# Which engine casts the first feed-forward products out of PSUM: ScalarE instead of VectorE in the first batch

## The chip, the cores and the metric

The kernel runs on one core of a Trainium2 chip. The metric is the device time of one execution in microseconds. The core has engines that run side by side, each working through its own queue in order: TensorE (PE; its weight loads are shown apart as PEld), VectorE (DVE), ScalarE (ACT), GpSimd (POOL) and SyncE (SP, which here issues transfers). They wait for one another through semaphores. TensorE writes its results to PSUM, an accumulator memory of eight banks per partition, and another engine has to read them out before a bank can be used again.

## The reference

Attention over hash buckets, followed by a feed-forward layer with a maximum of three products. There are 4 batches, 8 heads, 768 rows and 64 columns per head; every query attends only to the keys whose six sign bits (of a random projection) equal its own.

```python
q_bits = (np.einsum('bhsd,dk->bhsk', q, proj) > 0).astype(np.int64)
k_bits = (np.einsum('bhsd,dk->bhsk', k, proj) > 0).astype(np.int64)
...
scores = scale * np.matmul(q, k.transpose(0, 1, 3, 2))
scores = np.where(mask, scores, -1000000000.0)
...
attn = np.exp(scores)
attn = attn / (np.sum(attn, axis=-1, keepdims=True) + 1e-09)
out = np.matmul(attn, v)
...
h = np.maximum(np.maximum(x @ w1, x @ w2), x @ w3)
return (h @ w_out).astype(np.float32)
```

Here x is the attention output with the heads laid side by side: 3072 rows of 512; h has 768 columns.

## The kernel before

The queries are worked off in nine chunks: three of 256 queries in the first batch (`THIRD`), then two of 384 (`HALF`) in each of the other three. A chunk and a head are split into units: a unit is 768 columns of scores, three blocks of 256 in the first batch and two of 384 afterwards. There are 192 units, 48 in each batch.

**Scores.** For a unit, `scores` issues the score matmuls on TensorE (L298) into one of two score buffers in PSUM (`sc`), and one exponential on ScalarE (L306) that reads the whole buffer and writes a tile `AT`. As there are two buffers, the scores of a unit can start only when the exponential two units before has read its buffer.

**Bursts.** When four heads of a chunk are done, `burst` issues the sums of the exponentials (L358), their reciprocals on VectorE (L365 to L369), and the products with the values (L380); VectorE scales the result into `xT` (L387). From the fourth chunk on VectorE adds the exponentials up first (L329, L332).

**Feed-forward.** `ffn_groups` turns a finished chunk into a list of jobs. The first eighteen are products of a 128-column block `fb` of h with one of the three weights `wi`: four matmuls (L413) into one of four PSUM banks. What reads the bank depends on `wi`: for `wi` 0 the product is cast to float16 into a new tile `ht` (the lines that the change touches, L417 to L420); for `wi` 1 and 2 VectorE takes the maximum with `ht` in place (L422). In chunk 0 all six `wi` 0 jobs come first; in the others the three jobs of a block follow each other, so a cast comes with every third job. Then come the output products (L457), copied out by ScalarE (L461) and sent off by SyncE.

**Order.** It is written out by hand: each engine's instructions stand in its queue in the order in which the program issues them. The main loop runs over the units. For unit `u` it issues first the scores and the exponential of unit `u + 1`, then whatever is due at `u` (transposes of later inputs on VectorE at L202, loads, hashes), then the next feed-forward job or jobs, then bursts. One job falls due per unit in the first batch, 1.15 per unit after it. So a feed-forward job's matmuls stand on TensorE behind the scores of the next unit, and an instruction on ScalarE that reads the product stands behind the exponential of that unit and ahead of the exponential of the one after.

The jobs of chunks 0, 1 and 2, the first batch's, are worked off from 42 to 109 us, during the later units of the first batch and the units of the second. Their products are 256 columns wide, those of the other chunks 384.

Of the kernel before, what the change touches and what calls it, by code (L numbers as in the profile page):

```python
# [17 lines left out]
def kernel(  # L18
# [12 lines left out]
    nc = tc.nc  # L31
# [4 lines left out]
    HALF = S // 2  # L36
# [53 lines left out]
    def bank():  # L90
        i = free_banks.pop(0)
        return i, bank_tiles[i]

    def give(i):
        if i is not None:
            free_banks.append(i)
# [182 lines left out]
    def block_of(b, m):  # L279
        return 2 * (m % MH) + m // MH if b == 0 else m  # L280
# [34 lines left out]
    def xt_of(c):  # L315
        if c not in xts:
            xts[c] = x_pool.tile([P, NJC, HALF], FP16, tag="xT", name="xT")
        return xts[c]
# [83 lines left out]
    def ffn_groups(c):  # L402
        b, q0, w = chunks[c]
        xt = xt_of(c)
        hts, gs, l2 = {}, [], {}
        jobs = [(fb, wi) for fb in range(NFB) for wi in range(3)]
        if c == 0:
            jobs = [(fb, wi) for wi in range(3) for fb in range(NFB)]
        for fb, wi in jobs:
            def go(fb=fb, wi=wi):  # L410
                k_, ps = bank()
                for jc in range(NJC):
                    nc.tensor.matmul(ps[:, 0:w], w_sb[wi][:, jc, fb * P : (fb + 1) * P], xt[:, jc, 0:w],  # L413
                                     start=(jc == 0), stop=(jc == NJC - 1))
                if wi == 0:
                    hts[fb] = h_pool.tile([P, HALF], FP16, tag="ht", name="ht")
                    if w == HALF:  # L417
                        nc.scalar.copy(hts[fb][:, 0:w], ps[:, 0:w])  # L418
                    else:
                        nc.vector.tensor_copy(hts[fb][:, 0:w], ps[:, 0:w])  # L420
                else:
                    nc.vector.tensor_tensor(out=hts[fb][:, 0:w], in0=hts[fb][:, 0:w], in1=ps[:, 0:w], op=AluOp.max)  # L422
                give(k_)
            gs.append(go)
        rows = out[b * S : (b + 1) * S, :].rearrange("(p c) m -> c p m", c=NM)

        def out_rows(tb):
            if c < NCH - 1:
                return o_pool.tile([P, DM], FP32, tag="osb", name="osb")
            if "end" not in nat:  # L430
                nat["end"] = nat_pool.tile([P, 4 * NM * D], FP32, tag="nat", name="nat")
            return nat["end"][:, tb * DM : (tb + 1) * DM]

        def last(tb, cs, use_act):
            k_, ps = bank()
            n = cs.stop - cs.start
            for fb in range(NFB):
                nc.tensor.matmul(ps[:, 0:n], hts[fb][:, tb * P : (tb + 1) * P], wout_sb[:, fb, cs],  # L438
                                 start=(fb == 0), stop=(fb == NFB - 1))
            osb = out_rows(tb)  # L440
            if use_act:
                nc.scalar.copy(osb[:, cs], ps[:, 0:n])
            else:
                nc.vector.tensor_copy(osb[:, cs], ps[:, 0:n])
            give(k_)
            (nc.scalar if use_act else nc.sync).dma_start(rows[block_of(b, q0 // P + tb)][:, cs], osb[:, cs])

        def item(tb, part):
            def go2(part, tb=tb):
                if c == NCH - 1 and tb == w // P - 1:  # L450
                    last(tb, slice(part * DM // 2, (part + 1) * DM // 2), part == 0)
                    return
                if part == 0:
                    l2[tb] = bank()
                k_, ps = l2[tb]
                for fb in range(part * MH, (part + 1) * MH):
                    nc.tensor.matmul(ps[:, 0:DM], hts[fb][:, tb * P : (tb + 1) * P], wout_sb[:, fb, :],  # L457
                                     start=(fb == 0), stop=(fb == NFB - 1))
                if part == 1:
                    osb = out_rows(tb)  # L460
                    nc.scalar.copy(osb[:, 0:DM], ps[:, 0:DM])  # L461
                    give(k_)
                    nc.sync.dma_start(rows[block_of(b, q0 // P + tb)], osb[:, 0:DM])
            gs.append(lambda: go2(part))

        ntb = w // P
        steps = [(0, 0)]
        for tb in range(1, ntb):
            steps += [(tb, 0), (tb - 1, 1)]
        steps.append((ntb - 1, 1))  # L470
        if c == NCH - 1:
            steps = steps[:-3] + [steps[-2], steps[-3], steps[-1]]
        for tb, part in steps:
            item(tb, part)
        return gs
# [194 lines left out]
```

## Time and profile before

| | |
|---|---|
| median of three timed runs | 264.56 us (264.42 to 264.79) |
| the profiled execution | 264.41 us, span 262.4 us |
| TensorE matmul busy | 256.5 us (98% of the span) |
| VectorE busy | 207.8 us (79%) |
| ScalarE busy | 177.9 us (68%) |
| GpSimd busy | 69.8 us (27%) |
| granted TensorE clock | 1.000 |

The span runs from the first to the last instruction of the profiled execution; its time is some 2 us longer. A line such as "L306 ACT ACTIVATE AT<-sc 128x768 ... x192 | 152.4, 816 | 57.2" is a group: line of the program, engine, operation, what it writes and reads, shape and count, then its busy time in us, the mean of one in ns, and how long the engine had been idle just ahead of these instructions, with what ended that. A line of a timeline begins with the start in us and the duration in us; neighbouring instructions of one kind are merged, with their count after the x, and an idle time before them stands in brackets with what ended it. Instructions of one engine can overlap, so the next may start before the last one's duration is over; and since matmuls are pipelined, a group of them shows as longer than the time until the next group begins. Busy shares are averages over stages with different limits.

### The profile page before, as it was taken

What the parts mean: (1) busy time and instruction counts of PE and PEld (TensorE: products, weight loads), DVE (VectorE), ACT (ScalarE), POOL (GpSimd) and SP (SyncE); (2) the same over time, 40 slices, a digit from 0 to 9 for tenths busy, and PEclk for the clock granted to TensorE, in tenths of its full rate; (3) what the DMA queues carried; (4) which work ended last, traced back from release to release, by engine and by line L of the source; (5) the groups of instructions that cost most, each with busy time, mean ns of one, the idle gap of its engine ahead of it and who ended that gap; (6) DMA issues with size and microseconds to landing.
All of it is one profiled execution on the core that took longest, in us unless ns stands there. A gap on an engine that the chain in (4) does not pass through costs nothing.

```text
span 262.4 us, 6477 instructions
## 1 busy us (share of the span) xinstructions
PE 256.5 (98%) x2503; PEld 154.4 (59%) x2503; DVE 207.8 (79%) x492; ACT 177.9 (68%) x258; POOL 69.8 (27%) x132
## 2 busy tenths in 40 slices
PE   8999999999999999999999999999999999999995
PEld 4655658865765666555555554655555555555552
DVE  2897767966799999969999996899849795888350
ACT  3797886667968675956869588584886859581322
POOL 3878752355043526330141612011000000000000
PEclk9999999999999999999999999999999999999999
DMA  6998999979732964970073653802030003000303
GB/s 210 326 224 170 170 235 226 217 132 204 187 91 75 202 139 61 273 186 17 0 198 104 116 127 49 210 0 58 20 122 1 0 2 121 2 0 2 120 0 120
DMA packets 20717, 30.95 MB, mean 118 GB/s; under 512 B 2608, under 2 KB 15248, under 8 KB 20688
## 3 DMA queue, kind: packets, MB, share of 16 engines
q0 software_dynamic: 8128, 13.37, 27.3%
q1 hardware_dynamic: 12128, 16.66, 22.0%
q10 hardware_dynamic: 432, 0.52, 0.6%
q8 instruction: 19, 0.31, 0.5%
q14 instruction: 10, 0.08, 0.1%
HBM read 25.17 MB, written 6.29 MB: 120 GB/s over the span
## 4 chain that ended last, share of the span: by engine, by line
PE 89%; DVE 5%; ACT 3%; issue 2%; DVEq 0%; ACTq 0%
PE ms L413 34%; PE sc L298 22%; PE ms L457 11%; PE ms L380 10%; PE ms L221 3%; ACT AT L306 3%; PE ms L358 3%; PE ms L171 1%; PE ms L123 1%; PE ms L504 1%; DVE ht L422 1%; DVE ad L329 1%; DVE xT L387 1%; PE ms L150 1%; PE ms L438 1%
## 5 line engine op out<-in xcount | busy, mean ns | idle before, releaser
L306 ACT ACTIVATE AT<-sc 128x768 f16<-128x768 f32 x192 | 152.4, 816 | 57.2 <-PE sc L298 53.9
L413 PE MATMUL ms<-xT,w_sb 128*128 128x384 f16 (+1 forms) x648 | 115.0, 307 | 0.3 <-DVE xT L387 0.2
L298 PE MATMUL sc<-S 72*128 72x384 bf16 (+1 forms) x432 | 93.8, 308 | 1.2 <-ACT AT L306 0.9
L413 PEld LDWEIGHTS <-w_sb 128*128 128x128 f16 x648 | 62.7, 97 | 35.9 <-issue 0.4
L422 DVE TENSOR_TENSOR ht<-ht,ms 128x384 f16<-128x384 f16 (+1 forms) x108 | 54.2, 503 | 20.7 <-PE ms L413 10.5
L298 PEld LDWEIGHTS <-S 72*128 72x128 bf16 (+1 forms) x432 | 39.4, 98 | 31.8 <-issue 11.8
L207 POOL TENSOR_SCALAR T<-T 128x768 bf16<-128x768 f32 x24 | 22.8, 951 | 90.2 <-issue 48.4
L457 PE MATMUL ms<-wout_sb,ht 128*128 128x512 f16 x138 | 35.5, 378 | 0.0
L380 PE MATMUL ms<-AT,vo 128*32 128x385 f16 (+3 forms) x840 | 34.2, 308 | 0.0
L380 PEld LDWEIGHTS <-vo 128*32 128x32 f16 x864 | 22.9, 96 | 9.2 <-issue 1.7
L329 DVE TENSOR_TENSOR ad<-ad,AT 128x768 f16<-128x768 f16 x48 | 26.6, 553 | 2.1 <-ACT AT L306 1.3
L202 DVE STREAM_TRANSPOSE T<-nat 128x384 f32<-128x384 f32 x48 | 26.8, 564 | 0.0
L329 DVE TENSOR_TENSOR ad<-AT,AT 128x768 f16<-128x768 f16 x48 | 26.2, 546 | 0.2 <-ACT AT L306 0.2
L418 ACT CAST ht<-ms 128x384 f16<-128x384 f32 x36 | 17.3, 480 | 8.1 <-PE ms L413 8.1
L457 PEld LDWEIGHTS <-ht 128*128 128x128 f16 x138 | 13.3, 97 | 13.0 <-issue 0.3
L387 DVE SCALAR_TENSOR_TENSOR xT<-ms,sv,rb 128x384 f16<-128x384 f32 (+1 forms) x35 | 19.2, 565 | 1.3
L461 ACT COPY osb<-ms 128x512 f32<-128x512 f32 x21 | 12.2, 586 | 7.5 <-PE ms L457 5.8
L332 DVE TENSOR_TENSOR ad<-ad 128x384 f16<-128x384 f16 x32 | 15.5, 484 | 1.1
L137 POOL TENSOR_SCALAR S<-T 64x384 bf16<-64x384 f32 (+1 forms) x23 | 14.1, 616 | 4.9 <-DVE T L132 3.3
L196 POOL DMA_DIRECT2D nat<-in_q_dram x20 | 11.1, 560 | 0.1
L365 DVE STREAM_TRANSPOSE ys<-ms 128x384 f32<-128x384 f32 (+1 forms) x17 | 9.0, 531 | 2.3 <-PE ms L358 2.0
L176 DVE TENSOR_SCALAR S<-ms 6x384 bf16<-6x384 f32 x16 | 8.9, 554 | 2.0 <-PE ms L171 1.2
(52 smaller groups left out, 122.6 us busy)
## 6 DMA issues: line engine op xcount, KB each, us to landing
out_dram<-osb SPq DMA_DIRECT2D x21, 256.0 KB
S<-T SPq DMA_DIRECT2D x48, 96.0 KB
nat<-in_q_dram POOLq DMA_DIRECT2D x20, 192.0 KB, 6.3
vo<-in_v_dram POOLq DMA_DIRECT2D x8, 384.0 KB, 5.8
nat<-in_k_dram POOLq DMA_DIRECT2D x16, 192.0 KB, 5.7
w_sb<-in_moe_w_dram POOLq DMA_DIRECT2D x3, 768.0 KB, 12.8
nat<-in_k_dram SPq DMA_DIRECT2D x10, 192.0 KB
nat<-in_k_dram SPq DMA_DIRECT2D x3, 384.0 KB
```

The lines of the kernel that those rows point to most:

```text
L202: nc.vector.transpose(t32[name][:, u, half * HALF : (half + 1) * HALF], i_)
L207: nc.gpsimd.tensor_scalar(out=t16[name][:, u, :], in0=t32[name][:, u, :], scalar1=RS, scalar2=1.0, op0=AluOp.mult, op1=AluOp.mult)
L298: nc.tensor.matmul(views[j], s_of[kn][0 : D + bits, kx, m * P : (m + 1) * P], s_of[qn][0 : D + bits, qx, q0 : q0 + w], start=True, stop=True)
L306: nc.scalar.activation(t[:, :, 0:w], whole, ActFn.Exp, bias=-SCALE * 0.25 * bits, scale=SCALE)
L329: nc.vector.tensor_tensor(out=sum_of[c, h][:], in0=t[0], in1=t[n], op=AluOp.add)
L332: nc.vector.tensor_tensor(out=t[:, 0, :], in0=t[:, 0, :], in1=t[:, 1, :], op=AluOp.add)
L380: nc.tensor.matmul(av[Q * x : Q * (x + 1), 0:n], v_at[2 * b + i][:, x, cb * D + side : (cb + 1) * D : 2], weights_of(c, 4 * i + x, m)[:, 0 ...
L387: nc.vector.scalar_tensor_tensor(out=xt_of(c)[:, 2 * i + side, 0:w], in0=av[:, 0:w], scalar=sv_of[b, i, side][:], in1=rb[0][:, 0:w], op0=A ...
L413: nc.tensor.matmul(ps[:, 0:w], w_sb[wi][:, jc, fb * P : (fb + 1) * P], xt[:, jc, 0:w], start=(jc == 0), stop=(jc == NJC - 1))
L418: nc.scalar.copy(hts[fb][:, 0:w], ps[:, 0:w])
L422: nc.vector.tensor_tensor(out=hts[fb][:, 0:w], in0=hts[fb][:, 0:w], in1=ps[:, 0:w], op=AluOp.max)
L457: nc.tensor.matmul(ps[:, 0:DM], hts[fb][:, tb * P : (tb + 1) * P], wout_sb[:, fb, :], start=(fb == 0), stop=(fb == NFB - 1))
```

## The change

In the first batch's chunks the cast of the `wi` 0 product out of PSUM is issued on ScalarE and no longer on VectorE. In the other chunks it was on ScalarE before. Eighteen instructions of 128x256 change their engine; nothing else is moved, and the tile that they write and the bank that they read are the same.

```diff
                 if wi == 0:
                     hts[fb] = h_pool.tile([P, HALF], FP16, tag="ht", name="ht")
-                    if w == HALF:
-                        nc.scalar.copy(hts[fb][:, 0:w], ps[:, 0:w])
-                    else:
-                        nc.vector.tensor_copy(hts[fb][:, 0:w], ps[:, 0:w])
+                    nc.scalar.copy(hts[fb][:, 0:w], ps[:, 0:w])
                 else:
                     nc.vector.tensor_tensor(out=hts[fb][:, 0:w], in0=hts[fb][:, 0:w], in1=ps[:, 0:w], op=AluOp.max)
                 give(k_)
```

## The prediction

> **What bounds the kernel now.** I read the page first, then the busy time by windows, then what TensorE waited for, then the engines' timelines around the eighteen casts. From the page, the span and TensorE's total; one digit of the other rows is a fortieth of the span (6.56 us), in tenths busy:
>
> ```profile
> span 262.4 us, 6477 instructions
> ...
> PE   8999999999999999999999999999999999999995
> ...
> DVE  2897767966799999969999996899849795888350
> ACT  3797886667968675956869588584886859581322
> ```
>
> TensorE (PE) is full from the second slice to the last but one. VectorE (DVE) is in tenths 6 to 9 and ScalarE (ACT) 5 to 9 in the slices that hold the casts (7th to 17th, 43 to 105 us): each has room on the average. Waits of TensorE between 40 and 110 us, in total only this:
>
> ```profile
> PE ms L413 <- DVE xT L387: 0.2, 1, 0.2
> ```
>
> and two windows, each with its length and PE, PEld, DVE, ACT and POOL busy: the six casts of chunk 0, and a later stretch with casts of chunk 2:
>
> ```profile
> 43.00:47.50 4.50, 4.50 (x42) 3.82 (x40) 3.79 (x10) 4.50 (x7) 1.28 (x2) 1.00 1.19 239
> 86.00:100.50 14.50, 14.50 (x161) 9.53 (x163) 14.12 (x37) 10.14 (x14) 5.42 (x8) 1.00 0.67 148
> ```
>
> So the time is set by TensorE's own stream. An edit away from TensorE can gain only the little that TensorE loses to others, and it costs whatever it makes TensorE wait. VectorE's 14.12 of 14.50 us looks like the bound, but TensorE is at 14.50 of 14.50: VectorE is late there without holding anybody up. The first window is the opposite: ScalarE has 4.50 of 4.50, and that is where six casts go within seven exponentials.
>
> **What the change removes and adds.** Eighteen casts of 128x256 leave VectorE and join ScalarE's in-order queue, each right behind the exponential of the unit issued just before the product; matmuls, banks, transfers and the order of everything else stay. Group rows:
>
> ```profile
> L306 ACT ACTIVATE AT<-sc 128x768 f16<-128x768 f32 x192 | 152.4, 816 | 57.2 <-PE sc L298 53.9 <-POOL AT L395 2.1
> ...
> L418 ACT CAST ht<-ms 128x384 f16<-128x384 f32 x36 | 17.3, 480 | 8.1 <-PE ms L413 8.1
> ...
> L420 DVE CAST ht<-ms 128x256 f16<-128x256 f32 x18 | 7.4, 411 | 3.3 <-PE ms L413 3.3
> ...
> L442 ACT COPY nat<-ms 128x256 f32<-128x256 f32 x1 | 0.4, 372 | 0.1
> ```
>
> VectorE is relieved of 7.4 us, which is worth nothing except where TensorE waits for VectorE. ScalarE takes 18 casts of about 0.37 us (L442: same engine, same size, f32 out). What counts is the time that a cast adds between two exponentials, since neighbours overlap:
>
> ```profile
> 22.25 1.51 ACT L306 ACTIVATE AT<-sc 128x768 f16<-128x768 f32 x2 [0.69 <-PE sc L298]
> ...
> 123.95 0.81 ACT L306 ACTIVATE AT<-sc 128x768 f16<-128x768 f32 x1 [0.17 <-PE sc L298]
> 124.66 0.47 ACT L418 CAST ht<-ms 128x384 f16<-128x384 f32 x1
> 125.02 0.83 ACT L306 ACTIVATE AT<-sc 128x768 f16<-128x768 f32 x1
> ```
>
> Two exponentials take 1.51, so the second starts 0.70 to 0.71 after the first (1.51 - 0.81; 124.66 - 123.95). A cast of 384 columns adds 0.36 (125.02 - 124.66). The 256-column copy is 0.108 shorter than the 384-column cast (0.480 - 0.372): c = 0.25 us. Bounds: 0.24 if the 0.36 shrinks with the width (0.36 x 256/384), 0.37 if nothing overlaps. I take 0.25, since every such pair in the rows overlaps.
>
> The Trainium skill, "ScalarE: Activation LUTs", section "What ACT_TABLE_LOAD costs", gives an ACTIVATE with immediate scale and bias 186 ns + 0.833 ns per column, neighbours overlapping by 93 ns: c would be 0.31 (186 + 213 - 93), an estimate from that page. The trace's 384-column cast is a little under that formula (0.480 against 0.506); with 0.31 the sum below would be +1.07 instead of +0.65.
>
> **First stretch, chunk 0.** TensorE alternates score matmuls (L298) and one product (L413); ScalarE is close behind:
>
> ```profile
> 42.83 0.49 PE L298 MATMUL sc<-S 70*128 70x256 bf16 x3
> 43.16 0.60 PE L413 MATMUL ms<-xT,w_sb 128*128 128x256 f16 x4
> 43.59 0.49 PE L298 MATMUL sc<-S 70*128 70x256 bf16 x3
> ...
> 46.67 0.49 PE L298 MATMUL sc<-S 70*128 70x256 bf16 x3
> 47.00 0.60 PE L413 MATMUL ms<-xT,w_sb 128*128 128x256 f16 x4
> ```
>
> A unit takes TensorE 0.76 to 0.77 (43.59 - 42.83). On ScalarE:
>
> ```profile
> 41.91 6.09 ACT L306 ACTIVATE AT<-sc 128x768 f16<-128x768 f32 x8 [3.03 <-PE sc L298]
> ...
> 42.62 2.37 ACT L306 ACTIVATE AT<-sc 128x768 f16<-128x768 f32 x3
> ```
>
> ScalarE needs 0.71 for an exponential; with a cast 0.96, more than TensorE's 0.77. Two score buffers let TensorE run two units ahead, then the scores of a unit wait for the exponential two before it, starting 0.04 after it ends:
>
> ```profile
> 31.28 0.81 ACT AT L306
> ...
> 32.13 0.49 PE sc L298 x3
> ```
>
> Call the eight exponentials E1 to E8; E2 starts at 42.62. One cast follows each of E2 to E7; its product is always done by then (the first by 43.03, against 43.33 when ScalarE is free), so ScalarE runs without a gap. E6 starts at 42.62 + 4 x (0.707 + c), ends 0.81 later, and the scores of E8 (46.67 now) may start at 46.30 + 4c: 4c - 0.37 late, 0.63 us. After E8 TensorE has the sums and values of chunk 1 to do (some 2 us), in which ScalarE catches up; but TensorE has lost the time and has no idle time later to win it back.
>
> **Second stretch, chunk 1.** ScalarE is late here already, after two output copies:
>
> ```profile
> 64.33 0.81 ACT L306 ACTIVATE AT<-sc 128x768 f16<-128x768 f32 x1 [0.17 <-PE sc L298]
> 65.04 1.11 ACT L461 COPY osb<-ms 128x512 f32<-128x512 f32 x2
> 66.05 5.33 ACT L306 ACTIVATE AT<-sc 128x768 f16<-128x768 f32 x7
> ...
> 67.50 1.58 ACT L306 ACTIVATE AT<-sc 128x768 f16<-128x768 f32 x2
> ```
>
> ```profile
> 67.68 0.49 PE L298 MATMUL sc<-S 72*128 72x384 bf16 x2
> ...
> 69.98 0.49 PE L298 MATMUL sc<-S 72*128 72x384 bf16 x2
> ```
>
> One cast comes per three units, so excesses mostly drain. The first cast lies between the exponentials at 66.05 and 66.76: the latter starts at 66.76 + c, ends 0.81 later, and the scores of 67.68 start at 67.61 + c: 0.18 late. Their exponential, 0.59 behind the scores (68.27, the second of the pair from 67.50, against 67.68), is followed by the second cast; the next exponential starts at 67.86 + 0.59 + 0.71 + c = 69.41, ends at 70.22, and the scores of 69.98 start at 70.26: 0.28 in all (2c - 0.22). The later casts of this chunk fall before TensorE's burst at 73 us or where exponentials wait for scores anyway.
>
> **Third stretch, chunk 2.** The only tight place is around 92 us:
>
> ```profile
> 89.47 1.58 ACT L306 ACTIVATE AT<-sc 128x768 f16<-128x768 f32 x2 [2.47 <-PE sc L298]
> ```
>
> ```profile
> 92.01 0.49 PE L298 MATMUL sc<-S 72*128 72x384 bf16 x2
> ```
>
> The second of that pair starts at 90.24; a cast behind it puts the next at 90.95 + c, its end plus 0.04 at 91.80 + c, against 92.01: 0.04 late (c - 0.21).
>
> **What is given back.** One place where TensorE does wait for VectorE, for a bank:
>
> ```profile
> 79.17 0.41 DVE L420 CAST ht<-ms 128x256 f16<-128x256 f32 x1
> 79.50 0.56 DVE L202 STREAM_TRANSPOSE T<-nat 128x384 f32<-128x384 f32 x1
> 79.99 0.52 DVE L329 TENSOR_TENSOR ad<-ad,AT 128x768 f16<-128x768 f16 x1
> 80.42 0.41 DVE L422 TENSOR_TENSOR ht<-ht,ms 128x256 f16<-128x256 f16 x1
> ```
>
> ```profile
> 80.26 0.49 PE L298 MATMUL sc<-S 72*128 72x384 bf16 x2
> 80.89 0.60 PE L413 MATMUL ms<-xT,w_sb 128*128 128x256 f16 x4
> ```
>
> Two score matmuls occupy TensorE for 0.33 (a product follows scores by that much at 43.16), so the product could start at 80.59; it starts when the maximum of 80.42 to 80.83 has freed its bank: 0.30 lost. Without the cast at 79.17 that maximum is 0.33 earlier (79.50 - 79.17): the 0.30 comes back. The only other wait, 0.2 us for L387, lies ahead of the first cast and stays. Lower bound of this gain 0, upper 0.30.
>
> **Sum.** 0.63 + 0.28 + 0.04 - 0.30 = +0.65 us, in general 7c - 0.80 - 0.30. The profiled execution took 264.41 (2.0 outside its span), 0.15 under the median 264.56: 265.06 on that, 265.2 on the median. With c = 0.24 it is +0.58; with c = 0.37 +1.49, and +1.79 if the bank wait stays.
>
> **The rivals.**
>
> ScalarE swallows the casts (same, or a hair faster). One mechanism: a cast adds so little between exponentials that two score buffers cover it. It decides at c = 0.15 (under 0.21 the third term is nil, and 6c - 0.59 is then 0.30); at the floor (no stretch late, c under 0.09) only the regained 0.30 is left: 264.26. For it: ScalarE idles some 57 us before exponentials over the span, and L442 beats L420 (372 against 411 ns). Against it: no row has a cast adding under 0.36, which is 0.24 even if it shrinks with the width. Chance 0.25, mostly within the noise.
>
> The Trainium skill, "Advanced Engine Details and Errata", section "TRN2 Errata", says that ScalarE is closer to PSUM and VectorE to SBUF, to be used accordingly; by that rule this move should pay. The two rows just compared agree on the single copy; no row says that a shorter copy helps where ScalarE is the fuller engine. Its time would be the 264.26 of this rival.
>
> Casts don't overlap (slower, more): c = 0.37, 264.56 + 1.49 to 1.79 = 266.1 to 266.4. For it: a cast waits for another engine than the exponential ahead of it, and some wait for two. Against: the cast at 124.66 does too and overlaps. Chance 0.10.
>
> VectorE's maxima wait for casts. In chunks 1 and 2 the first maximum of a block follows its cast by one unit. Behind a waiting maximum stand transposes, adds of exponentials and the sums' reciprocals, for which TensorE's bursts wait. A cast one exponential late ends 0.71 + 0.37 after its product, a maximum's own product is 0.77 after it: 0.31 late, twelve times 3.7 us, against 12 x 0.33 regained on VectorE. Only a ScalarE lateness of more than one exponential makes a net loss; for each further 0.1, 1.2 us: 266.4 with the sum above. For it: VectorE is at 14.12 of 14.50. Against: the two score buffers keep ScalarE from falling that far behind. Chance 0.05.
>
> **How the numbers follow.** Forecast 0.60, at 265.2. About 0.2% (0.53 us) is what a measurement can tell here. Slower by more: the forecast less the part of its spread under +0.53 (0.07), and the two dear rivals, 0.68; within 0.2%: 0.28; faster: 0.04, as even the floor of the first rival is -0.30. The range 264.6 to 266.3 reaches down into the absorbing case and up to the no-overlap price.
>
> **What would show it.** Scores of the eighth unit in the first stretch starting some 0.6 us late, exponentials there 0.96 apart with casts between; TensorE's L298 waiting for ScalarE L306 at about 45 to 47.5 and again near 68 and 70.5; the gap ahead of the product at 80.9 closed; VectorE's busy sum 7.4 lower, ScalarE's some 6.7 higher; from 106 us on the same timeline, shifted. Wrong: no wait of L298 for L306 in the first stretch (c misjudged), a wait of L358 for VectorE (a late burst), or a gap in TensorE after 106 us.

## The result and the profile after

The changed kernel took 266.16 us (median of four runs, 265.57 to 266.26) against 264.53 us for the kernel before (four runs, 264.42 to 264.79): ratio 1.0053, 95% interval 1.0036 to 1.0071. The profiled execution took 265.57 us.

From the page of the changed kernel, span, totals and the rows in fortieths of the span (6.59 us each):

```profile
span 263.7 us, 6478 instructions
...
PE 257.7 (98%) x2503; PEld 154.4 (59%) x2503; DVE 201.9 (77%) x474; ACT 181.4 (69%) x276; POOL 69.8 (26%) x132
...
PE   8999999999999999999999999999999999999995
...
DVE  2797767567599899768999996899949785788361
ACT  3797886776969685965869589484885859581322
```

VectorE's total fell by 5.9 us (18 instructions fewer), ScalarE's rose by 3.5 and TensorE's by 1.2 us with the same 2503 matmuls. The prediction had 7.4 and 6.7 for the first two: it took sums of durations, and the totals count the time once in which two instructions of an engine overlap. The span is 1.3 us longer. Two groups of ScalarE, kept apart by shape, with busy time and mean of one:

```profile
L306 ACT ACTIVATE AT<-sc 128x768 f16<-128x768 f32 x192 | 153.6, 821 | 55.1 <-PE sc L298 51.6 <-POOL AT L395 2.1 <-ACT AT L306 0.2
...
L417 ACT CAST ht<-ms 128x256 f16<-128x256 f32 x18 | 7.2, 400 | 0.0
```

ScalarE idles for nothing ahead of the casts: each finds its product ready. They take 400 ns in the mean, not 372, and the exponentials 821, not 816. The two windows of the prediction, with length and PE, PEld, DVE, ACT, POOL busy:

```profile
43.00:47.50 4.50, 4.39 (x36) 3.40 (x36) 1.74 (x4) 4.50 (x10) 1.49 (x2) 1.00 1.19 234
86.00:100.50 14.50, 14.50 (x155) 9.58 (x154) 12.82 (x31) 10.86 (x20) 4.86 (x8) 1.00 0.60 148
```

In the first, VectorE went from 3.79 to 1.74 us, ScalarE stayed full, and TensorE has 36 matmuls instead of 42: that is the loss, in the place where the prediction put it. In the second TensorE is full as before. TensorE's waits between 40 and 110 us, however, are listed as before:

```profile
PE ms L413 <- DVE xT L387: 0.2, 1, 0.2
```

By this list alone the prediction's own sign against it, no wait of L298 for L306 in the first stretch, would have been met. But the new stalls are too short for this view. A product's four matmuls are on record for 0.60 us, but the next matmul can start 0.44 after their first; a stall of 0.21 leaves 0.05 of idle time on record. So I laid the starts of TensorE's matmuls beside those of before, one by one, and noted where the lateness grows. Steps in us, each the change of the median lateness across the place (times of before; "133" is the last of the sums ahead of L380, at 131.9 before, 133.3 after):

| kernel | chunk 0, 44 to 47 | chunk 1, 67 to 70 | bank, 80.9 | chunk 2, 92 | sums, 133 | ratio to before, 95% interval |
|---|---|---|---|---|---|---|
| predicted | +0.63 | +0.28 | -0.30 | +0.04 | 0 | |
| the change | +0.72 | +0.34 | -0.31 | +0.06 | +0.29 | 1.0053 [1.0036, 1.0071] |
| again | +0.72 | +0.34 | -0.31 | +0.06 | +0.28 | 1.0047 [1.0034, 1.006] |
| chunk 0 alone | +0.72 | 0 | 0 | 0 | 0 | 1.0025 [1.0015, 1.0036] |
| chunks 1 and 2 | 0 | +0.34 | -0.30 | +0.06 | 0 | 1.001 [0.9999, 1.002] |
| one cast | 0 | 0 | -0.30 | 0 | 0 | 0.9989 [0.9979, 0.9999] |
| cast twice | +2.33 | 0 | -0.01 | 0 | 0 | 1.009 [1.0074, 1.0107] |
| cast halved | +0.30 | 0 | -0.01 | 0 | 0 | 1.0013 [1.0002, 1.0023] |
| last two | 0 | 0 | 0 | 0 | 0 | 0.9994 [0.9983, 1.0006] |
| 16 memsets | +0.73 | +0.34 | -0.31 | +0.06 | 0 (+0.22 at 174) | 1.0036 [1.0025, 1.0048] |
| 22 memsets | +0.72 | +0.34 | -0.30 | +0.06 | 0 | 1.0043 [1.0021, 1.0066] |
| 10 memsets | +0.78 | +0.34 | -0.30 | +0.06 | 0 | 1.0022 [1.001, 1.0034] |
| 11 memsets | +0.72 | +0.34 | -0.31 | +0.07 | +0.29 | 1.0043 [1.0026, 1.006] |

The row of the change adds up to +1.10. Two differences belong to single executions and to no edit: the lateness at 20 to 35 us, +0.22 here and between -0.19 and +0.61 over these runs, and -0.06 at 139.8 us in every row, so that it is the profile of before that stands apart there. With both, 1.10 + 0.22 - 0.06 = 1.26 us, the 1.3 by which the span grew.

TensorE in the first stretch of the changed kernel; the five groups of scores of chunk 0 after the first cast:

```profile
43.81 0.49 PE L298 MATMUL sc<-S 70*128 70x256 bf16 x3
...
44.67 0.49 PE L298 MATMUL sc<-S 70*128 70x256 bf16 x3
44.99 0.60 PE L413 MATMUL ms<-xT,w_sb 128*128 128x256 f16 x4
45.65 0.49 PE L298 MATMUL sc<-S 70*128 70x256 bf16 x3
...
46.63 0.49 PE L298 MATMUL sc<-S 70*128 70x256 bf16 x3
...
47.61 0.49 PE L298 MATMUL sc<-S 70*128 70x256 bf16 x3
```

The units are 0.98 apart (45.65 - 44.67, 46.63 - 45.65, 47.61 - 46.63) where they were 0.77 apart before. ScalarE in the same stretch, start and duration:

```profile
43.77 0.84 ACT L306 ACTIVATE AT<-sc 128x768 f16<-128x768 f32 x1
44.48 0.41 ACT L417 CAST ht<-ms 128x256 f16<-128x256 f32 x1
44.73 0.87 ACT L306 ACTIVATE AT<-sc 128x768 f16<-128x768 f32 x1
45.43 0.43 ACT L417 CAST ht<-ms 128x256 f16<-128x256 f32 x1
45.68 0.90 ACT L306 ACTIVATE AT<-sc 128x768 f16<-128x768 f32 x1
...
48.54 0.98 ACT L306 ACTIVATE AT<-sc 128x768 f16<-128x768 f32 x1
```

Their starts follow the forecast: a cast 0.71 behind its exponential, the next exponential 0.25 behind the cast. But each exponential is on record about 0.03 longer than the one ahead (0.84, 0.87, 0.90, up to 0.98; why is not known), so the ends are not 0.96 but some 0.98 apart, and it is the end that frees a score buffer: 44.73 + 0.87 = 45.60, and the scores start at 45.65.

The product that had waited for its bank at 80.89 no longer does; it follows its scores by 0.32 where it was 0.63 before:

```profile
80.77 0.49 PE L298 MATMUL sc<-S 72*128 72x384 bf16 x2
81.09 0.60 PE L413 MATMUL ms<-xT,w_sb 128*128 128x256 f16 x4
```

The step ahead of the sums at 133 us was not foreseen. TensorE there, first before and then in the changed kernel:

```profile
131.93 0.35 PE L358 MATMUL ms<-ad,ones 128*32 128x384 f16 x4
132.11 2.15 PE L380 MATMUL ms<-AT,vo 128*32 128x385 f16 x48
```

```profile
132.97 0.63 PE L358 MATMUL ms<-ad,ones 128*32 128x384 f16 x4
133.28 1.33 PE L380 MATMUL ms<-AT,vo 128*32 128x385 f16 x27
```

The sums (four matmuls over `ad`, which VectorE adds up at L329 and L332) take 0.63 instead of 0.35: the last of them waits for the last `ad`. VectorE had no idle time of its own from some 10 us earlier on, where this stands:

```profile
122.30 0.55 DVE L419 TENSOR_TENSOR ht<-ht,ms 128x384 f16<-128x384 f16 x1
123.31 0.55 DVE L419 TENSOR_TENSOR ht<-ht,ms 128x384 f16<-128x384 f16 x1 [0.46 <-PE sc L298]
123.78 0.55 DVE L329 TENSOR_TENSOR ad<-AT,AT 128x768 f16<-128x768 f16 x1
```

Between the first maximum's end (122.85) and the next one's start lie 0.46 us, where it is 0.10 in the versions that have no stall at 133. The releaser in the brackets is only the last event ahead of the start; in the list of VectorE's records the semaphore wait of this maximum is done at 122.91, and its record comes 396 ns after that, where 45 ns is usual. That record is the 319th of VectorE's, counted from nought, and the page counts all instruction transfers of the smaller kind under one queue:

```profile
q14 instruction: 10, 0.08, 0.1%
```

One of these 8 KB transfers follows the late maximum 0.7 us later, at 123.99. In the kernel before the 319th record is late as well: it is the maximum at 114.32, 396 ns behind its semaphore wait, and VectorE idles soon after it. The change took 20 records out of VectorE's stream (640 instead of 660), so that the 319th became the maximum at 123.31, behind which VectorE has no idle time until the sums.

### The profile page after: what moved, and what is told of

It reads as the page before. It is cut to its first block, busy times and chain, and to the rows that moved or that the text cites. A ratio compares the mean times of both kernels' runs of the same rounds, so it can differ in the third digit from the quotient of the medians.

```text
span 263.7 us, 6478 instructions
## 1 busy us (share of the span) xinstructions
PE 257.7 (98%) x2503; PEld 154.4 (59%) x2503; DVE 201.9 (77%) x474; ACT 181.4 (69%) x276; POOL 69.8 (26%) x132
## 4 chain that ended last, share of the span: by engine, by line
PE 91%; ACT 5%; issue 1%; DVE 1%; ACTq 0%
PE ms L413 35%; PE sc L298 23%; PE ms L454 11%; PE ms L380 11%; ACT AT L306 4%; PE ms L221 3%; PE ms L358 3%; PE ms L123 1%; PE ms L171 1%; PE ms L501 1%; PE ms L150 1%; PE ms L435 1%; ACT T L130 1%; ACT ht L417 0%; DVE xT L387 0%
## 5 line engine op out<-in xcount | busy, mean ns | idle before, releaser
L306 ACT ACTIVATE AT<-sc 128x768 f16<-128x768 f32 x192 | 153.6, 821 | 55.1 <-PE sc L298 51.6
L298 PE MATMUL sc<-S 72*128 72x384 bf16 (+1 forms) x432 | 93.7, 308 | 1.4 <-ACT AT L306 0.9
L298 PEld LDWEIGHTS <-S 72*128 72x128 bf16 (+1 forms) x432 | 39.4, 98 | 32.8 <-issue 12.9
L380 PE MATMUL ms<-AT,vo 128*32 128x385 f16 (+3 forms) x840 | 34.4, 308 | 0.0
L417 ACT CAST ht<-ms 128x384 f16<-128x384 f32 (+1 forms) x54 | 24.5, 454 | 8.1 <-PE ms L413 8.1
L380 PEld LDWEIGHTS <-vo 128*32 128x32 f16 x864 | 23.0, 96 | 9.3 <-issue 1.9
L329 DVE TENSOR_TENSOR ad<-ad,AT 128x768 f16<-128x768 f16 x48 | 26.6, 555 | 2.0 <-ACT AT L306 1.3
L329 DVE TENSOR_TENSOR ad<-AT,AT 128x768 f16<-128x768 f16 x48 | 26.5, 553 | 0.2 <-ACT AT L306 0.2
L387 DVE SCALAR_TENSOR_TENSOR xT<-ms,sv,rb 128x384 f16<-128x384 f32 (+1 forms) x35 | 19.2, 565 | 1.4
L332 DVE TENSOR_TENSOR ad<-ad 128x384 f16<-128x384 f16 x32 | 15.5, 484 | 1.1
```

What stands on the lines that cost most here:

```text
L298: nc.tensor.matmul(views[j], s_of[kn][0 : D + bits, kx, m * P : (m + 1) * P], s_of[qn][0 : D + bits, qx, q0 : q0 + w], start=True, stop=True)
L306: nc.scalar.activation(t[:, :, 0:w], whole, ActFn.Exp, bias=-SCALE * 0.25 * bits, scale=SCALE)
L329: nc.vector.tensor_tensor(out=sum_of[c, h][:], in0=t[0], in1=t[n], op=AluOp.add)
L332: nc.vector.tensor_tensor(out=t[:, 0, :], in0=t[:, 0, :], in1=t[:, 1, :], op=AluOp.add)
L380: nc.tensor.matmul(av[Q * x : Q * (x + 1), 0:n], v_at[2 * b + i][:, x, cb * D + side : (cb + 1) * D : 2], weights_of(c, 4 * i + x, m)[:, 0 ...
L387: nc.vector.scalar_tensor_tensor(out=xt_of(c)[:, 2 * i + side, 0:w], in0=av[:, 0:w], scalar=sv_of[b, i, side][:], in1=rb[0][:, 0:w], op0=A ...
```

## The experiments

Two questions were open: whether the steps follow from ScalarE's lateness as the terms of the prediction have them, and where the 0.29 us ahead of the sums come from: from VectorE waiting for later casts on ScalarE, or from the place of its instructions in its own stream. The diffs are against the changed kernel.

### The changed kernel again

No edit.

> The changed kernel once more, unaltered. Theory A (ScalarE's rate against two score buffers): TensorE's stream shows the same four late score starts of chunk 0 (+0.10, +0.21, +0.21, +0.21 us), two in chunk 1 (+0.22, +0.13), one in chunk 2 (+0.07), and the regained bank wait at 81 us (-0.31), in all +0.83 us; what is beyond that, up to the measured +1.6 us of the median, lies elsewhere and differs from run to run. Theory B (VectorE, made to wait for ScalarE, arrives late at a later burst): the +0.29 us ahead of the sums at 133 us comes again, at the same place. Time 266.0 to 266.2.

265.76 us (six runs), below the 266.0 to 266.2 expected, with the same five steps, the last of them (0.28) at the same instruction: not a chance of one execution.

### Chunk 0 alone

```diff
-                    nc.scalar.copy(hts[fb][:, 0:w], ps[:, 0:w])
+                    if w == HALF or c == 0:
+                        nc.scalar.copy(hts[fb][:, 0:w], ps[:, 0:w])
+                    else:
+                        nc.vector.tensor_copy(hts[fb][:, 0:w], ps[:, 0:w])
```

> Only chunk 0's six casts are on ScalarE; those of chunks 1 and 2 stay on VectorE as before. Theory A: +0.73 us in the first stretch and nothing else, the bank wait at 81 us stays: 265.2 to 265.3. Theory B: in chunk 0 no maximum follows close on its cast, so VectorE's later lateness does not arise; also +0.73, and whatever the change costs beyond +0.8 is missing here.

265.12 us. Only chunk 0's step is there. The bank wait at 80.9 stays, and there is no stall at 133.

### Chunks 1 and 2 alone

```diff
-                    nc.scalar.copy(hts[fb][:, 0:w], ps[:, 0:w])
+                    if c > 0:
+                        nc.scalar.copy(hts[fb][:, 0:w], ps[:, 0:w])
+                    else:
+                        nc.vector.tensor_copy(hts[fb][:, 0:w], ps[:, 0:w])
```

> Only the twelve casts of chunks 1 and 2 are on ScalarE; chunk 0's stay on VectorE. Theory A: +0.34 and +0.07 late scores, -0.31 for the bank wait: +0.10 us, 264.6. Theory B: the unexplained rest of the change (some 0.8 us of its median) is here: 265.3 to 265.5, with a wait of TensorE for VectorE at a burst after 110 us.

264.83 us. The steps of chunks 1 and 2 and the regained bank wait are there, which nearly cancel (0.34 - 0.30 + 0.06 = +0.10), and no stall at 133, although all casts that VectorE could be waiting for between 64 and 109 us are on ScalarE as in the change. So that stall is not a wait for ScalarE. It needs both halves, which fits a count of instructions and not a wait for any one of them.

### One cast

```diff
-                    nc.scalar.copy(hts[fb][:, 0:w], ps[:, 0:w])
+                    if w == HALF or (c == 1 and fb == 4):
+                        nc.scalar.copy(hts[fb][:, 0:w], ps[:, 0:w])
+                    else:
+                        nc.vector.tensor_copy(hts[fb][:, 0:w], ps[:, 0:w])
```

> Only one cast, of block 4 in chunk 1, is on ScalarE. Theory A: ScalarE idles behind it, so no score is late, and VectorE is 0.33 us earlier where TensorE waited 0.30 us for a bank at 81 us: -0.30 us, 264.2 to 264.3, faster than both kernels. If the bank wait had another cause than VectorE's queue: 264.5, the wait still there.

264.12 us (twelve runs), against 264.53 of the kernel before (27 runs). ScalarE takes the one cast where it has room, and the product of 80.9 follows its scores at once; ScalarE first, then TensorE:

```profile
77.15 0.81 ACT L306 ACTIVATE AT<-sc 128x768 f16<-128x768 f32 x1
77.86 0.37 ACT L418 CAST ht<-ms 128x256 f16<-128x256 f32 x1
```

```profile
80.06 0.49 PE L298 MATMUL sc<-S 72*128 72x384 bf16 x2
80.39 0.60 PE L413 MATMUL ms<-xT,w_sb 128*128 128x256 f16 x4
```

It is the only version clear of the kernel before on the fast side, by 0.3 us in the trace; the interval of its ratio just excludes 1.

### 16 memsets ahead

```diff
+        for _ in range(16):
+            nc.vector.memset(ones[:, 0:2], 1.0)
```

They stand at the start of VectorE's stream, where `ones` is set anyway, and set the same value.

> The changed kernel with sixteen tiny VectorE memsets (of a constant that is already set) at the start, where VectorE waits for a load; nothing else differs. In the changed kernel a maximum at 123 us starts 0.35 us after all that it waits for; it is VectorE's 319th record, and an 8 KB transfer of the instruction queue follows 0.7 us later. Theory C (the hitch belongs to a position in VectorE's instruction stream): with sixteen records ahead of it, position 319 falls on an instruction ahead of which VectorE idles 1.4 us, the hitch is hidden, and TensorE's wait of 0.29 us ahead of the sums at 133 us is gone: 0.29 us under the changed kernel, ratio to before about 1.003. Theory B (a wait for ScalarE): the hitch stays at the same maximum and the time is that of the changed kernel, ratio 1.0045 to 1.005.

265.55 us, a ratio of 1.0036 where 1.003 was expected. The gap at the maximum is gone, and so is the stall at 133. But another one of 0.22 us came 41 us later, with a gap of the same kind ahead of VectorE's record 447, which is 319 + 128:

```profile
166.78 0.58 DVE L369 STREAM_TRANSPOSE rb<-rr 128x384 f32<-128x384 f32 x1
167.85 1.14 DVE L387 SCALAR_TENSOR_TENSOR xT<-ms,sv,rb 128x384 f16<-128x384 f32 x2 [0.48 <-PE sc L298]
```

### Chunk 0 cast twice

The six casts of chunk 0 are issued twice in a row on ScalarE with the same values; those of chunks 1 and 2 are on VectorE.

```diff
-                    nc.scalar.copy(hts[fb][:, 0:w], ps[:, 0:w])
+                    if w == HALF or c == 0:
+                        nc.scalar.copy(hts[fb][:, 0:w], ps[:, 0:w])
+                    else:
+                        nc.vector.tensor_copy(hts[fb][:, 0:w], ps[:, 0:w])
+                    if c == 0:
+                        nc.scalar.copy(hts[fb][:, 0:w], ps[:, 0:w])
```

> Chunk 0's six products are each cast twice on ScalarE into the same tile; chunks 1 and 2 as before the change. A cast and an exponential took 0.980 us from end to end in the changed kernel, the exponential alone 0.707: c is 0.273 there. Theory A: the first stretch is late by 4 x 0.546 - 0.37 = 1.8 us in TensorE's stream, nothing elsewhere: 266.3. Rival (a fixed loss at the hand-over between engines, not ScalarE's rate): 0.73 as with single casts, 265.2.

266.86 us; the step of chunk 0 was 2.33, more than expected. ScalarE:

```profile
44.10 0.82 ACT L306 ACTIVATE AT<-sc 128x768 f16<-128x768 f32 x1
44.80 0.38 ACT L418 CAST ht<-ms 128x256 f16<-128x256 f32 x1
45.22 0.37 ACT L422 CAST ht<-ms 128x256 f16<-128x256 f32 x1
45.48 0.82 ACT L306 ACTIVATE AT<-sc 128x768 f16<-128x768 f32 x1
```

The second cast starts only when the first is over (44.80 + 0.38 = 45.18): no overlap between these two, presumably because both write the same tile, which was not tried. A unit takes 1.38 (45.48 - 44.10), so the pair adds 1.38 - 0.707 = 0.673, and 4 x 0.673 - 0.37 = 2.32. The form of the term holds, with a cost read off this same run; the expectation had the wrong cost of the second cast. The exponentials do not lengthen here (0.82 each), although ScalarE is further behind than in the changed kernel. Stalls this long are seen in TensorE's list of waits, between 40 and 110 us, though with 1.7 of the 2.33 us:

```profile
PE sc L298 <- ACT AT L306: 1.7, 4, 0.5
```

### Chunk 0 cast by halves

ScalarE casts columns 0 to 127, VectorE the others; chunks 1 and 2 are on VectorE.

```diff
-                    nc.scalar.copy(hts[fb][:, 0:w], ps[:, 0:w])
+                    if c == 0:
+                        nc.scalar.copy(hts[fb][:, 0:P], ps[:, 0:P])
+                        nc.vector.tensor_copy(hts[fb][:, P:w], ps[:, P:w])
+                    elif w == HALF:
+                        nc.scalar.copy(hts[fb][:, 0:w], ps[:, 0:w])
+                    else:
+                        nc.vector.tensor_copy(hts[fb][:, 0:w], ps[:, 0:w])
```

> Chunk 0's six casts are split: the first 128 columns on ScalarE, the other 128 on VectorE; chunks 1 and 2 as before the change. Theory A: at 0.9 ns per column c falls by 0.116 to 0.157 us, and the stretch is late by 4 x 0.157 - 0.37 = 0.26 us: 264.8. Rival (fixed loss): 0.73, 265.2.

264.83 us, step +0.30. ScalarE:

```profile
43.54 0.84 ACT L306 ACTIVATE AT<-sc 128x768 f16<-128x768 f32 x1
44.24 0.30 ACT L418 CAST ht<-ms 128x128 f16<-128x128 f32 x1
44.39 0.87 ACT L306 ACTIVATE AT<-sc 128x768 f16<-128x768 f32 x1
```

Starts 0.85 apart, and again records that lengthen by 0.03 from one to the next: 0.87 to 0.88 by the ends, so a cast of 128 columns adds 0.166 and 4 x 0.166 - 0.37 = 0.29. That is 0.107 less than for 256 columns, 0.84 ns per column.

### The last two casts of chunk 0

```diff
-                    nc.scalar.copy(hts[fb][:, 0:w], ps[:, 0:w])
+                    if w == HALF or (c == 0 and fb >= 4):
+                        nc.scalar.copy(hts[fb][:, 0:w], ps[:, 0:w])
+                    else:
+                        nc.vector.tensor_copy(hts[fb][:, 0:w], ps[:, 0:w])
```

> Of chunk 0's six casts only the last two are on ScalarE; all others as before the change. Theory A: the late scores come from the casts behind the second to fifth exponential, and behind the last two TensorE has some 2 us of sums and values to do: no late scores, 0.00 us, 264.5. Rival (each cast on ScalarE costs its share): a third of 0.73, +0.24 us, 264.8.

264.61 us and no step at all. Lateness has to add up over several units before the two score buffers pass it on; the last two casts come too late for that.

### 22, 10 and 11 memsets

As with 16, with another count. They were sent to see whether the count decides where the late record falls (theory C) or any extra work at the start does the same (rival D).

> The changed kernel with 22 further two-column memsets of a constant on VectorE near the start (they set a value that is there already). Theory C (VectorE's position in its instruction stream: one record in 128 comes late if nothing is queued): counted in the trace of the changed kernel, the late records now fall 22 instructions earlier, on the maximum at 114.3 us, which VectorE's idle time right behind it absorbs, and on L224 at 165.7 us, which has waited 2.8 us for something else anyway. So no wait of TensorE ahead of the sums at 133 us and none at 173 to 174 us; the steps ahead of that as in the changed kernel (+0.73, +0.34, -0.31, +0.07, sum +0.83); about 265.3 us, ratio 1.003. Rival D (any extra work at the start removes the wait at 133 us and brings one at 173 us, whatever its count): as with 16 memsets, none at 133 us, +0.23 at 173 to 174 us, ratio 1.0036 or more.

No stall at 133 and none at 174, as C has it; D wanted one at 174. The time, 265.75 us, is above the 265.3 expected, with a wide interval (five runs); its profiled execution was already 0.61 late at 20 us.

> The same with 10 memsets. Theory C: the late records fall on the first L387 at 119.9 us (behind a semaphore wait, so a gap of about 0.4 us ahead of it instead of 0.05) and on L202 at 169.0 us, which is ready and queued behind others. VectorE has no idle time between 120 and 132 us, so the wait of TensorE ahead of the sums at 133 us comes back, 0.2 to 0.35 us, and there is none at 173 to 174 us; about 265.5 us, ratio 1.004 to 1.005. Rival D: as with 16 memsets, none at 133 us, +0.23 at 173 to 174 us.

265.29 us; no stall at either place, where C wanted the one at 133 back. (The profiled execution lost another 0.28 us between 35 and 43 us, ahead of nearly all casts; this was not traced.) The list of records shows why: the first memset took over a semaphore wait that had been a record of its own, so the stream had moved by nine and not by ten, and the 319th record was a semaphore wait in the shadow of a running L387. It came 0.36 us late and nobody noticed. D fell too: it wanted a stall at 174. Which record is hit was then counted anew and tried with one memset more:

> The changed kernel with 11 memsets of a constant at the start of VectorE's stream. With 10, the late record (the 319th, counted from nought) was a semaphore wait in the shadow of the first L387, because the first memset took over a semaphore wait that had been a record of its own: memsets shift the stream by their count less one. With 11 the 319th is the first L387 itself, behind a semaphore wait at about 120 us. Theory C: a gap of about 0.40 us ahead of that L387 instead of 0.05, VectorE that much late until 132 us, and TensorE waits 0.2 to 0.35 us ahead of the sums at 133 us again; the 447th is an L202 that is queued behind others, so no wait at 173 to 174 us. Rival D (the wait at 133 us goes with any padding): no wait at 133 us, as with 10, 16 and 22 memsets. By the steps the time is 1.1 us over the kernel before under C, 0.83 us under D.

265.63 us. VectorE, and below it TensorE at the sums:

```profile
119.23 0.58 DVE L369 STREAM_TRANSPOSE rb<-rr 128x384 f32<-128x384 f32 x1
120.27 1.14 DVE L387 SCALAR_TENSOR_TENSOR xT<-ms,sv,rb 128x384 f16<-128x384 f32 x2 [0.46 <-PE ms L380]
```

```profile
132.96 0.63 PE L358 MATMUL ms<-ad,ones 128*32 128x384 f16 x4
```

The gap has moved to the L387 that was named beforehand (396 ns behind its semaphore wait), the maximum at 122.65 follows without one, and the sums take 0.63 again: the step of 0.29 is back. One memset fewer, and it is gone:

```profile
133.23 0.35 PE L358 MATMUL ms<-ad,ones 128*32 128x384 f16 x4
```

## Why the prediction was right, and where it was not

**The bound.** Right. TensorE's stream sets the time; 5.9 us less on VectorE were worth the 0.31 us of one bank wait.

**The first stretch, 4c - 0.37.** Mechanism and place right, one size off. The step was put at 0.63 and measured at 0.72, because c was read off the distance between starts (0.25), while the score buffer is freed at the end of an exponential. In this stretch the records lengthen from one to the next, and the distance of the ends is 0.98: c = 0.98 - 0.707 = 0.273, and 4 x 0.273 - 0.37 = 0.72. The halved and doubled casts bear the term out with c read off each of these runs, and the last two casts alone, which the term leaves out, cost nothing. The formula of the Trainium skill, "ScalarE: Activation LUTs", section "What ACT_TABLE_LOAD costs", by which c was estimated at 0.31, is above what the trace shows.

**The second and third stretch, 2c - 0.22 and c - 0.21.** Right in place. With c = 0.273 they give 0.33 and 0.06, measured 0.34 and 0.06.

**What is given back, -0.30.** Right: -0.31, and -0.30 with that one cast alone on ScalarE.

**The sum.** 7c - 0.80 - 0.30 with c = 0.273 is +0.81; the four steps measured give 0.72 + 0.34 + 0.06 - 0.31 = +0.81. The prediction had +0.65; the 0.16 that it lacks are seven times the 0.023 by which its c was too small.

**The step that was missing.** From 106 us on the timeline was to be the same, shifted. It was not: 0.29 us ahead of the sums at 133, a wait of L358 for VectorE, which the prediction had named as a sign against it, though as a late burst. It follows from the change in a way that no term had: with casts gone from VectorE's stream, its later instructions moved up in their count, and one that TensorE depends on came to stand where a record comes late. Shown is that it depends on the count: with 0 and 11 memsets it is there, with 10, 16 and 22 it is not, and with 11 it was foretold to the instruction. The same late record stands at two more places 128 apart: the 191st with 11 memsets (a maximum at 73.83 us, 409 ns behind its semaphore wait) and the 575th with chunk 0 alone (a maximum at 221.90 us, 414 ns). Both cost TensorE nothing. That the fetching of instructions is behind it is argued only from the distance of 128 and from the 8 KB transfers; it was not tried by itself. A transfer comes 0.7 us after the late record here and 1.5 us after it with 16 memsets, so it is not what that record waited for. The 0.29 us are read from traces alone: the medians do not separate the versions with the stall from those without it (ratio 1.0043 with 11 memsets and with 22).

**The rivals.** That ScalarE swallows the casts fell for chunk 0 and holds for single ones: the cast at 77.86 in the version with one cast, and the last two of chunk 0. That casts don't overlap fell: 0.25 from start to start, and 0.41 only where a cast was made to wait for the one ahead. That VectorE's maxima wait for the casts fell with chunks 1 and 2 alone, which cost 0.10 us. The shorter single copy on ScalarE (372 against 411 ns), with which the rule of the Trainium skill, "Advanced Engine Details and Errata", section "TRN2 Errata", agrees, did not decide: the change is slower.

**The time.** The forecast was 265.2 us, +0.65; the median of 266.16 is +1.63. It lies inside the range of 264.6 to 266.3, but near its upper end, which is the price of casts that don't overlap, and they do. So the direction and the places were foreseen; that the range held is partly luck, since the step at 133 was in no term.

Against the median the sum of the steps, 1.10 - 0.06, is 1.0039 of 264.53 us; the two measurements of the changed kernel have 1.0036 to 1.0071 and 1.0034 to 1.006. What is between that and their middles lies within the intervals and stays open: the profiled execution was the fastest of its four, and the 0.6 us more of the other three (266.12 to 266.26) left no trace.

## What to carry to other kernels

Ask which engine is full in the very stretch where an instruction lands, not over the span: between two score buffers an engine may fall behind by a fixed amount, and a short instruction per unit costs nothing until that is used up, and from then on all that it adds between two others. Take the cost of an instruction inserted into a backlog from the distance of ends, since ends free buffers. And when a move works in one place and costs in three, make it in the one place: one cast of eighteen gave the whole gain. If an edit changes the number of instructions of an engine, a cost that has nothing to do with it may move with the count; a few instructions more or less show that.

## What the runs showed of the hardware

VectorE's records at positions 191, 319, 447 and 575 of its stream, 128 apart, can come some 0.35 us late (396 to 414 ns behind a semaphore wait instead of 45). It is seen where the record ahead is a semaphore wait and VectorE has nothing else under way; it is hidden where an instruction runs meanwhile (the record in the shadow of L387 with 10 memsets) or where VectorE idles anyway. It cost TensorE 0.29 us at 319 in the changed kernel, about a third of the 0.81 us that the casts themselves cost, and 0.22 us at 447 with 16 memsets. The Trainium skill, "Runtime: NRT & Kernel Launch", section "Instruction fetch mechanics", holds that fetching is hidden behind the rate at which instructions are issued; if it is fetching that shows here, it was not hidden in these runs.

ScalarE's records can grow in a row of exponentials and casts in which each starts before the one ahead has ended: exponentials from 0.84 to 0.98 us and casts from 0.38 to 0.51 over six units, with unchanged distances from start to start. Being behind is not enough: with each cast issued twice, where the second waits for the first, the exponentials stay at 0.82. What makes them grow is open.

The first 20 us of an execution vary by up to 0.8 us from one to the next (from -0.19 to +0.61 against the profile of before), more than most of the edits here cost or bring.
